# Attention and gated feed-forward on one core: one batch of attention, and chunk 0 alone, ahead of the fast chunks

## The chip, the cores and the metric

One core of one Trainium2 chip. The metric is the device time of one launch in microseconds (us), on the chip; several executions of each kernel were timed, and medians are quoted. The span of a profile is a little shorter than the timed run that it belongs to (1127.2 against 1129.3 us for the kernel before), so spans are compared with spans and timed runs with timed runs. The outputs of all kernels below were correct.

## The reference

```python
def _attn_ref(q, k, v, g_norm):                     # (8 batches, 8 heads, 576, 64), float32
    kv = np.einsum('bhsd,bhse->bhde', k, v)
    out = np.einsum('bhsd,bhde->bhse', q, kv)
    rms = np.sqrt(np.mean(out * out, axis=-1, keepdims=True) + 1e-06)
    return (out / rms * g_norm).astype(np.float32)

def _moe_ref(x, w_gate, w_val, w_out):              # 4608 tokens, d_model 512, d_ff 1536
    gate = 1.0 / (1.0 + np.exp(-(x @ w_gate)))
    val = x @ w_val
    return (gate * val @ w_out).astype(np.float32)

# x of the second is the first's result, heads side by side; the three weights are float64
```

## The kernel before

Words used below:

- A **pair** is two heads of attention. A batch has four pairs. A pair's steps on TensorE are kv (k times v), q (transposes of q), u (q times kv) and x (transposes of the normed u); each is followed by a step of ScalarE or VectorE. The last one, `x_out`, writes the pair's part of `xT`, the input of the feed-forward.
- A **chunk** is 512 tokens, nine in all. Chunk 0 needs batch 0 alone, chunk 1 batches 0 and 1.
- A **unit** is 1024 float64 weights in each of 128 partitions, which VectorE (DVE) and ScalarE (ACT) turn into float32 in five **conversion steps**: 12 units of gate and value weights (one for each f of 128 columns of d_ff), then 6 of w_out.
- A **block** (c, f) is the first layer of chunk c for one f: eight 512-column matmuls, then a sigmoid of the gate half on ACT and the product of both halves on DVE.
- "**Seven products**" is a Strassen-like scheme of the later chunks: seven quarter-size products in place of eight, for some added and subtracted quarters (of x on DVE, of the gate and value weights on GpSimd (POOL), of w_out once).
- A **slot** is a place between two matmuls at which one waiting step of the next batch's attention, or one sum, is emitted. Every engine takes its instructions in the order in which they are emitted.
- **Half clock**, or a **cold** array: stretches in which PE takes twice as long for like work. The same ten u records took 2.48 us early in the kernel after and 1.26 later (10.57 and 28.71 us); at full clock the array is called **warm**. The **granted clock** of a view is 1.00 at full and 0.50 at half clock.

The order in which the conversion steps are queued, each turn of a block, and the old plan: eight pairs, then chunks 0 and 1 block by block.

```python
    halves_of = [convert(u) for u in range(len(units))]   # per unit: ([s0, s1], [s2, s3, s4])
    converts, last = deque(), {}
    converts.extend(halves_of[0][0] + halves_of[0][1] + halves_of[1][0])
    last[0] = 5
    for u in range(1, len(units)):
        if u + 1 < len(units):
            converts.extend(halves_of[u + 1][0])
        converts.extend(halves_of[u][1])
        last[u] = len(converts)
    # ... (convert_some(n) emits the next n steps; s0, s1: a DVE step and an ACT step each;
    #      s2, s3, s4: DVE alone; s4 also starts the load of a later unit)

    def plain(c, f, n_convert, ps):
        converted(f)
        blk = Plain(c, f, ps)
        for at in range(2 * NMT):                         # eight matmuls
            i, m = divmod(at, NMT)
            blk.mm(i, m)
            slot()
            if late:
                late.popleft()()                          # gate and product of the block before
            convert_some(n_convert * (at + 1) // 8 - n_convert * at // 8)
        late.extend([blk.gate, blk.end])

    def stage(i, n_convert):                              # four pairs under way at a time
        do(i, KV, Q, KV_OUT, Q_OUT)
        do(i - 2, U_SUM, U_ROOT, U_NORM)
        do(i - 1, U, U_SQUARE)
        do(i - 3, X, X_OUT)
        convert_some(n_convert)

    for i in range(NE + 1):                               # NE = 8 pairs
        stage(i, 2 if i < 2 else 1 if i == 2 else 0)
    # ... block (0, 0), the last pair's last steps
    blocks = [(1, 0)] + [(c, f) for f in range(1, NFT - 3) for c in range(2)] + [(0, f) for f in range(NFT - 3, NFT)]
    for n, (c, f) in enumerate(blocks):
        plain(c, f, 5, halves(two(n % 4)))
    finish()
    convert_some(len(converts))
    # ...
    tt(out=t2w[3], in0=b22, in1=b12, op=ALU.subtract)     # a sum of w_out's quarters
    feed(2, at_ps)                                        # queue batch 2's steps for the slots
    second_layer(0)                                       # t outermost, f innermost
    # ...
    for f in range(NFT - 3, NFT):
        plain(1, f, 0, (mm_ps(), mm_ps()))
        # ... the other three sums of w_out's quarters, the sums of the hidden layer
    flush()
    sums_of(2)
    second_layer_fast(1)                                  # seven products
    flush()
    for c in range(2, NG):
        if c + 1 < B:
            feed(c + 1, at_ps)
        first_layer_fast(c)                               # seven products
        sums_of(c + 1)
        second_layer_fast(c)
        flush()
```

## Time and profile before

| | kernel before |
|---|---|
| timed runs | 1130.72 us median of 3 (1128.84 to 1131.5) |
| span of the profile | 1127.2 us |
| eight pairs and blocks (0,0), (1,0) end, block (0,1) starts | 59.55 us |
| second layer of chunk 0 starts | 190.25 us |
| chunk 2 starts (from here on both kernels are the same) | 301.72 us |

The milestones are read from the chain of work that ended last: the first matmul of each part. The third stretch, from chunk 0's second layer to chunk 2, in columns: stretch, length, then busy time of TensorE (PE), its weight loads (PEld), DVE, ACT and POOL, granted clock, share of the DMA engines, GB/s:

```profile
190.25:301.72 111.47, 110.26 (x494) 70.09 (x493) 33.55 (x65) 24.50 (x42) 0.00 (x0) 1.00 0.19 49
```

PE loses 1.2 us of 111 here. So outside of the first 59.55 us the old kernel has nearly nothing left to win by better overlap; only work can be taken away.

### The profile page before, as it was taken

To read this page: it belongs to the slowest core of one execution; us is meant where nothing else is said; L and a number is where in the kernel's file an instruction comes from. 1 tells how busy PE (TensorE), PEld (TensorE's weight loads), DVE (VectorE), ACT (ScalarE), POOL (GpSimd) and SP (SyncE) were. 2 spreads that over 40 slices of the span, in tenths; PEclk is the share of its full clock that TensorE was granted. 3 is DMA by queue.
4 is the path that set the end of the run, shared out by engine and by line. 5 is a ranking of instruction groups with operands and counts; after the bars stand their busy time and mean duration, and the time that the engine had idled before them with its cause. 6 is when DMAs were issued, how large, how long until landed. Compare 5 with 4: busy or idle time off the path is not lost.

```text
span 1127.2 us, 14586 instructions
## 1 busy us (share of the span) xinstructions
PE 1106.3 (98%) x5616; PEld 884.9 (79%) x5616; DVE 536.6 (48%) x1087; ACT 310.5 (28%) x589; POOL 239.5 (21%) x342
## 2 busy tenths in 40 slices
PE   5999999999999999999999999999999999999998
PEld 5644444547888888888888888888888888888887
DVE  4577664054155524563355425551655246615641
ACT  3733330223033303331243113340334021101110
POOL 0000001000033303430133104420333034404420
PEclk9999999999999999999999999999999999999999
DMA  9944431220212012110202030201200000010001
GB/s 239 216 133 131 147 112 28 55 71 12 75 26 54 11 29 63 42 34 19 72 12 54 24 78 12 53 12 40 56 12 7 19 19 1 1 26 13 1 1 38
DMA packets 71588, 57.56 MB, mean 51 GB/s; under 512 B 40800, under 2 KB 65376, under 8 KB 71520
## 3 DMA queue, kind: packets, MB, share of 16 engines
q1 hardware_dynamic: 71360, 56.64, 19.1%
q8 instruction: 45, 0.74, 0.3%
q14 instruction: 23, 0.19, 0.1%
q10 hardware_dynamic: 160, 0.00, 0.0%
HBM read 47.19 MB, written 9.44 MB: 50 GB/s over the span
## 4 chain that ended last, share of the span: by engine, by line
PE 94%; DMA 2%; DVE 2%; ACT 1%; SPq 0%; issue 0%; DVEq 0%
PE mm L526 45%; PE mm L606 26%; PE two L400 9%; PE mm L385 4%; PE at L400 3%; PE at L256 2%; PE at L227 2%; DMA q<-in_q_dram 1%; PE at L241 1%; PE at L282 1%; PE mm L400 1%; DMA v<-in_v_dram 1%; PE two L256 0%; DVE sq L273 0%; DVE ms L264 0%; ACT gv L141 0%
## 5 line engine op out<-in xcount | busy, mean ns | idle before, releaser
L512 POOL TENSOR_TENSOR tw<-gv 128x256 f32<-128x256 f32 x168 | 120.7, 730 | 836.8 <-PE mm L526 655.6
L526 PE MATMUL mm<-sx,tw 128*128 128x256 f32 x672 | 159.7, 380 | 0.0
L526 PE MATMUL mm<-xT,tw 128*128 128x256 f32 x672 | 159.5, 380 | 0.0
L526 PE MATMUL mm<-xT,gv 128*128 128x256 f32 x672 | 158.7, 379 | 0.0
L526 PEld LDWEIGHTS mm<-xT,gv 128*128 128x128 f32 x672 | 127.7, 190 | 17.4
L526 PEld LDWEIGHTS mm<-sx,tw 128*128 128x128 f32 x672 | 126.1, 190 | 16.7
L526 PEld LDWEIGHTS mm<-xT,tw 128*128 128x128 f32 x672 | 125.3, 190 | 16.1
L512 POOL TENSOR_TENSOR tw<-gv,tw 128x256 f32<-128x256 f32 x168 | 123.8, 760 | 0.0
L400 PE MATMUL two<-xT,gv 128*128 128x512 f32 x256 | 111.3, 593 | 2.1 <-DVE gv L163 1.6
L400 PEld LDWEIGHTS two<-xT,gv 128*128 128x128 f32 x256 | 48.3, 190 | 62.4 <-issue 62.1
L606 PE MATMUL mm<-t2w,gv 128*128 128x256 f32 x384 | 89.0, 379 | 0.0
L606 PE MATMUL mm<-w,gv 128*128 128x256 f32 x384 | 88.1, 379 | 0.0
L606 PE MATMUL mm<-w,s 128*128 128x256 f32 x384 | 88.1, 379 | 0.0
L555 ACT ACTIVATE sg<-sg 128x256 f32<-128x256 f32 x84 | 35.0, 416 | 191.7 <-DVE sg L554 191.7
L606 PEld LDWEIGHTS mm<-w,s 128*128 128x128 f32 x384 | 73.0, 190 | 9.9
L606 PEld LDWEIGHTS mm<-t2w,gv 128*128 128x128 f32 x384 | 72.6, 190 | 9.7
L606 PEld LDWEIGHTS mm<-w,gv 128*128 128x128 f32 x384 | 72.5, 190 | 9.6
L526 PE MATMUL mm<-sx,gv 128*128 128x256 f32 x336 | 79.4, 379 | 0.0
L546 DVE TENSOR_TENSOR gv<-mm,sg 128x256 f32<-128x256 f32 x84 | 35.7, 425 | 88.9 <-PE mm L526 88.9
L533 ACT COPY sg<-mm 128x256 f32<-128x256 f32 x84 | 31.3, 372 | 141.0 <-PE mm L526 141.0
L526 PEld LDWEIGHTS mm<-sx,gv 128*128 128x128 f32 x336 | 63.1, 190 | 8.2
L562 DVE TENSOR_TENSOR gv<-gv,sg 128x512 f32<-128x512 f32 x84 | 67.2, 840 | 0.2
(93 smaller groups left out, 1151.0 us busy)
## 6 DMA issues: line engine op xcount, KB each, us to landing
k<-in_k_dram SPq DMA_DIRECT2D x32, 288.0 KB, 4.4
v<-in_v_dram SPq DMA_DIRECT2D x32, 288.0 KB, 5.1
q<-in_q_dram SPq DMA_DIRECT2D x64, 144.0 KB, 3.1
st<-in_moe_w_gate_dram SPq DMA_DIRECT2D x12, 512.0 KB, 3.9
st<-in_moe_w_val_dram SPq DMA_DIRECT2D x12, 512.0 KB, 5.3
st<-in_moe_w_out_dram SPq DMA_DIRECT2D x12, 512.0 KB, 4.0
out_dram<-sg SPq DMA_DIRECT2D x24, 192.0 KB, 2.3
out_dram<-sg SPq DMA_DIRECT2D x24, 128.0 KB, 2.3
```

The source lines that it names most:

```text
L227: nc.tensor.matmul(ps[HD * e:HD * e + HD, 0, 0:HD], pairs[n]["k"][:, e, js], pairs[n]["v"][:, e, js], start=(j == 0), stop=(j == NJ - 1))
L241: nc.tensor.transpose(ps[:, j // JH, c0:c0 + NP], pairs[n]["q"][:, j].rearrange("p e d -> p (e d)"), ident[0:NP, 0:NP])
L256: nc.tensor.matmul(d["u"][:, i], qT[:, M * i:M * i + MU], kvs[n % 2], start=True, stop=True)
L385: nc.tensor.matmul(ps, gv[c, f][:, P * t:P * t + P], w["wo", f], start=(f == 0), stop=(f == NFT - 1))
L400: nc.tensor.matmul(self.ps[i], w[("wg", "wv")[i], self.f][:, m, :], xT[self.c][:, m, :], start=(m == 0), stop=(m == NMT - 1), skip_group_c ...
L512: nc.gpsimd.tensor_tensor(out=tw[f, i], in0=b[in0], in1=b[in1] if isinstance(in1, tuple) else tw[f, in1], op=ALU.subtract)
L526: nc.tensor.matmul(ps, wt[:, m, :], xs[:, m, :], start=(new and m == 0), stop=(m == NK - 1), skip_group_check=True)
L533: nc.scalar.copy(out=d["sg"][:, h2], in_=pa)
L546: tt(out=d["h"][:, h2], in0=pb, in1=d["sg"][:, h2], op=ALU.add)
L555: nc.scalar.activation(out=d["sg"][:, h2], in_=d["sg"][:, h2], func=AF.Sigmoid)
L562: tt(out=d["h"], in0=d["h"], in1=d["sg"], op=ALU.mult)
L606: nc.tensor.matmul(ps, hs(f), ws[:, f, :], start=(new and f == 0), stop=(f == NF2 - 1), skip_group_check=True)
```

## The change

The intent is to take work from PE. Chunk 1's first layer was plain, because its blocks lay between chunk 0's as company for the conversion. Now chunk 0 alone goes with the conversion, and chunk 1 is the first of the fast chunks. So only batch 0 is needed before block (0,0), and batch 1 goes into the slots of chunk 0. The second layer of chunk 0 gets f outermost, since w_out is still being converted. The core of the diff:

```diff
-    NE = 2 * NHP
+    NE = NHP
...
-    converts.extend(halves_of[0][0] + halves_of[0][1] + halves_of[1][0])
-    last[0] = 5
-    for u in range(1, len(units)):
-        if u + 1 < len(units):
+    for u in range(len(units)):
+        if u <= 4:
+            converts.extend(halves_of[u][0])
+        if 4 <= u < len(units) - 1:
             converts.extend(halves_of[u + 1][0])
         converts.extend(halves_of[u][1])
...
-            slot()
+            if at % 2:
+                slot()
             if late:
                 late.popleft()()
-            convert_some(n_convert * (at + 1) // 8 - n_convert * at // 8)
+            if 0 < at < 7:
+                convert_some(1)
...
-    for i in range(NE + 1):
-        stage(i, 2 if i < 2 else 1 if i == 2 else 0)
... (the start, now pair by pair:)
+    do(0, KV, Q, KV_OUT, Q_OUT, U, U_SQUARE, U_SUM, U_ROOT)
+    convert_some(2)
+    do(0, U_NORM, X, X_OUT)
+    convert_some(1)
+    do(1, KV, Q, KV_OUT, Q_OUT, U, U_SQUARE)
+    convert_some(2)
+    do(1, U_SUM, U_ROOT)
+    do(2, KV, Q, KV_OUT, Q_OUT)
+    do(1, U_NORM)
+    blk.mm(0, 0)
...
-    blocks = [(1, 0)] + [(c, f) for f in range(1, NFT - 3) for c in range(2)] + [(0, f) for f in range(NFT - 3, NFT)]
-    for n, (c, f) in enumerate(blocks):
-        plain(c, f, 5, halves(two(n % 4)))
+    plain(0, 1)
+    feed(1, at_ps)
+    for f in range(2, NFT):
+        plain(0, f)
+    ps = [mm_ps() for _ in range(G // P)]
+    for f in range(NFT - 2):
+        if f % 2 == 0:
+            converted(NFT + f // 2)
+        for t in range(G // P):
+            second(t, f)
+            if t % 2:
+                slot()
+            ...
+            if t < 3:
+                convert_some(1)
+    flush()
+    convert_some(len(converts))
...
+    fill.extend(x_sums(1))
... (second(t, f) for the last two f, copies and stores)
+    def t2w_sum(i, in0, in1):
+        for fs in (slice(0, NF2 // 2), slice(NF2 // 2, NF2)):
+            fill.append(lambda fs=fs: tt(out=t2w[i][:, fs], in0=in0[:, fs], in1=in1[:, fs], op=ALU.subtract))
+    t2w_sum(3, b22, b12)
+    t2w_sum(1, b12, b11)
+    t2w_sum(2, b22, t2w[1])
+    t2w_sum(4, b21, t2w[2])
-    for c in range(2, NG):
+    for c in range(1, NG):
```

More of the change, by code (lines that the diff above doesn't have):

```diff
@@ L64 @@
     first = first_ctx.__enter__()
-    NE = 2 * NHP
+    NE = NHP
     pairs = {n: {} for n in range(B * NHP)}
-    def ahead(n, late):
-        return (n + 4,) if n + 4 < NE else (n + late,) if n + late >= NE else ()
     def load_kv(n):
@@ L163, in s4 @@
             vec.tensor_tensor(out=m, in0=m, in1=d["p"].bitcast(FP32), op=ALU.mult)
-            if u:
-                load_next_unit()
+            load_next_unit()
         return [s0, s1], [s2, s3, s4]
@@ L187, in converted @@
         convert_some(last[u] - made[0])
-    for n in range(4):
+    for n in range(NE):
         load_kv(n)
@@ L193 @@
             load_next_unit()
+    load_next_unit()
+    load_next_unit()
     w2 = const.tile([P, NFT, DM], FP32, name="w2")
@@ L233, in kv_out @@
                 nc.vector.tensor_copy(out=kvs[n % 2][es, es], in_=d["kv"][es, 0, 0:HD])
-            for i in ahead(n, 2):
-                load_kv(i)
+            if n + 2 >= NE:
+                load_kv(n + 2)
         def q_mm():
@@ L246, in q_out @@
             nc.scalar.copy(out=d["qT"], in_=d["q"][:, :, 0:JH * NP])
-            for i in ahead(n, 1):
-                load_q(i)
+            if n + 1 >= NE:
+                load_q(n + 1)
         def u_mm():
@@ L358, in at_ps, with early, ps @@
         return psum_at.tile([P, 2, 512], FP32, tag="at", name="at")
-    def two(i):
-        return at_ps(None) if i == 3 else psum0.tile([P, 2, 512], FP32, tag=f"two{i}", name="two")
-    shared = [None]
-    turns = {"u": 1, "qx": 0}
-    def early(kind):
-        if kind == "q":
-            return shared[0]
-        tag = "u" if kind == "u" else "qx"
-        t = two(turns[tag] if tag == "u" else 2 + turns[tag])
-        turns[tag] = 1 - turns[tag]
-        if kind == "kv":
-            shared[0] = t
-            return t[:, :, JH * P:]
-        return t
+    def early(n):
+        shared = []
+        def ps(kind):
+            if kind == "q":
+                return shared[0]
+            t = psum0.tile([P, 2, 512], FP32, tag="kq" if kind == "kv" else f"ux{n % 2}", name="two")
+            if kind == "kv":
+                shared.append(t)
+                return t[:, :, JH * P:]
+            return t
+        return ps
     def mm_ps():
         return psum.tile([P, 512], FP32, tag="mm", name="mm", bufs=6)
-    def second_layer(c):
-        for t in range(G // P):
-            ps = mm_ps()
-            for f in range(NFT):
-                nc.tensor.matmul(ps, gv[c, f][:, P * t:P * t + P], w["wo", f], start=(f == 0), stop=(f == NFT - 1))
-                if f % 2:
-                    slot()
-            ot = sg_tile()
-            nc.scalar.copy(out=ot, in_=ps)
-            store(c, t, ot)
     class Plain:
@@ L410, with plain @@
     late = deque()
-    def finish():
-        while late:
-            late.popleft()()
-    def halves(t):
-        return t[:, 0], t[:, 1]
-    def plain(c, f, n_convert, ps):
+    def plain(c, f):
         converted(f)
-        blk = Plain(c, f, ps)
+        blk = Plain(c, f, (mm_ps(), mm_ps()))
         for at in range(2 * NMT):
@@ L425, in plain @@
             blk.mm(i, m)
-            slot()
+            if at % 2:
+                slot()
             if late:
                 late.popleft()()
-            convert_some(n_convert * (at + 1) // 8 - n_convert * at // 8)
+            if 0 < at < 7:
+                convert_some(1)
         late.extend([blk.gate, blk.end])
     KV, KV_OUT, Q, Q_OUT, U, U_SQUARE, U_SUM, U_ROOT, U_NORM, X, X_OUT = range(11)
-    a = [attention(n, early) for n in range(NE)]
+    a = [attention(n, early(n)) for n in range(NE)]
@@ L436, in do @@
     def do(n, *steps):
-        if 0 <= n < NE:
-            for step in steps:
-                a[n][step]()
-    def stage(i, n_convert):
-        do(i, KV, Q, KV_OUT, Q_OUT)
-        do(i - 2, U_SUM, U_ROOT, U_NORM)
-        do(i - 1, U, U_SQUARE)
-        do(i - 3, X, X_OUT)
-        convert_some(n_convert)
-    for i in range(NE + 1):
-        stage(i, 2 if i < 2 else 1 if i == 2 else 0)
-        if i + 5 == NE:
-            load_next_unit()
-            load_next_unit()
-    blk = Plain(0, 0, halves(early("u")))
@@ L454 @@
-    for m in range(NMT):
-        blk.mm(0, m)
-    do(NE - 1, U_SUM, U_ROOT)
-    do(NE - 2, X, X_OUT)
-    do(NE - 1, U_NORM)
-    convert_some(2)
-    for m in range(2):
-        blk.mm(1, m)
-    do(NE - 1, X, X_OUT)
-    for m in range(2, NMT):
-        blk.mm(1, m)
-    convert_some(2)
-    blk.gate()
+        for step in steps:
+            a[n][step]()
+    at0 = at_ps(None)
+    blk = Plain(0, 0, [at0[:, i] for i in range(2)])
+    do(0, KV, Q, KV_OUT, Q_OUT, U, U_SQUARE, U_SUM, U_ROOT)
@@ new lines @@
+    convert_some(2)
+    do(0, U_NORM, X, X_OUT)
+    convert_some(1)
+    do(1, KV, Q, KV_OUT, Q_OUT, U, U_SQUARE)
+    convert_some(2)
+    do(1, U_SUM, U_ROOT)
+    do(2, KV, Q, KV_OUT, Q_OUT)
+    do(1, U_NORM)
+    blk.mm(0, 0)
+    do(2, U, U_SQUARE, U_SUM, U_ROOT)
+    do(1, X, X_OUT)
+    blk.mm(1, 0)
+    do(3, KV, Q, KV_OUT, Q_OUT)
+    do(2, U_NORM)
+    blk.mm(0, 1)
+    do(3, U, U_SQUARE, U_SUM, U_ROOT)
+    do(2, X, X_OUT)
+    blk.mm(1, 1)
+    convert_some(1)
+    do(3, U_NORM)
@@ L467 @@
+    blk.mm(0, 2)
+    blk.mm(1, 2)
+    do(3, X, X_OUT)
+    convert_some(4)
+    blk.mm(0, 3)
+    blk.mm(1, 3)
+    late.extend([blk.gate, blk.end])
     first_ctx.__exit__(None, None, None)
     hp = ctx.enter_context(tc.tile_pool(name="hp", bufs=21))
-    blk.end()
-    blocks = [(1, 0)] + [(c, f) for f in range(1, NFT - 3) for c in range(2)] + [(0, f) for f in range(NFT - 3, NFT)]
-    for n, (c, f) in enumerate(blocks):
-        plain(c, f, 5, halves(two(n % 4)))
-    assert n % 4 == 3
-    finish()
@@ L475, with second @@
-    convert_some(len(converts))
     psum_ctx.__exit__(None, None, None)
     psum = ctx.enter_context(tc.tile_pool(name="psum", bufs=1, space=bass.MemoryType.PSUM))
+    plain(0, 1)
[3 more added lines that the diff above has]
+    ps = [mm_ps() for _ in range(G // P)]
+    def second(t, f):
+        nc.tensor.matmul(ps[t], gv[0, f][:, P * t:P * t + P], w["wo", f], start=(f == 0), stop=(f == NFT - 1),
+                         skip_group_check=True)
+    for f in range(NFT - 2):
[5 more added lines that the diff above has]
+                slot()
+            if late:
+                late.popleft()()
+            if t < 3:
+                convert_some(1)
@@ L635 @@
     sums = ctx.enter_context(tc.tile_pool(name="sums", bufs=2, side="right"))
+    for n in (1, 2, 3, 4):
+        for f in (0, NF2):
+            w_sum(f, n)
+    fill.extend(x_sums(1))
+    for t in range(G // P):
+        for f in range(NFT - 2, NFT):
+            second(t, f)
+            slot()
+        ot = sg_tile()
+        nc.scalar.copy(out=ot, in_=ps[t])
+        store(0, t, ot)
     b12, b11, b21, b22 = (w2[:, NF2 * (j - 1):NF2 * j, DH * (n - 1):DH * n] for j, n in ((1, 2), (1, 1), (2, 1), (2, 2)))
@@ L638 @@
     t2w[1] = b12
-    tt(out=t2w[3], in0=b22, in1=b12, op=ALU.subtract)
-    feed(2, at_ps)
-    second_layer(0)
-    for n in (1, 2, 3, 4):
-        for f in (0, NF2):
-            w_sum(f, n)
-    for f in range(NFT - 3, NFT):
-        plain(1, f, 0, (mm_ps(), mm_ps()))
-        if f == NFT - 3:
-            tt(out=t2w[1], in0=b12, in1=b11, op=ALU.subtract)
-            tt(out=t2w[2], in0=b22, in1=t2w[1], op=ALU.subtract)
-            tt(out=t2w[4], in0=b21, in1=t2w[2], op=ALU.subtract)
-            for i in range(NF2 - 3):
-                h_sums(1, i)
-    finish()
-    for i in range(NF2 - 3, NF2):
-        h_sums(1, i)
-    flush()
-    sums_of(2)
-    second_layer_fast(1)
-    flush()
-    for c in range(2, NG):
+    def t2w_sum(i, in0, in1):
[6 more added lines that the diff above has]
+    for c in range(1, NG):
         if c + 1 < B:
```

## The prediction

> **What bounds the kernel now.** I read the page first (busy shares, slices), then the chain of waits, then the stretches between its milestones, then the timeline of the first 75 us.
>
> ```profile
> PE 1106.3 (98%) x5616; PEld 884.9 (79%) x5616; DVE 536.6 (48%) x1087; ACT 310.5 (28%) x589; POOL 239.5 (21%) x342
> PE   5999999999999999999999999999999999999998
> DVE  4577664054155524563355425551655246615641
> ```
>
> TensorE (PE) is busy in 98% of 1127.2 us, and only its first slice is thin. So time is won by less PE work, or by less PE idling at the start. The chain gives the milestones: block (0,1), the first that needs weight unit 1, starts at 59.55; chunk 0's second layer at 190.25; chunk 2 at 301.72. From there on the two kernels have the same program, 825.5 us long.
>
> ```profile
> 0.00:59.55 59.55, 43.74 (x393) 32.89 (x393) 30.21 (x59) 31.28 (x58) 0.70 (x6) 1.00 0.93 216
> 59.55:190.25 130.70, 130.70 (x305) 57.99 (x306) 86.59 (x97) 42.32 (x49) 5.52 (x8) 1.00 0.34 112
> 301.72:422.53 120.81, 120.81 (x685) 106.56 (x685) 56.87 (x130) 34.98 (x71) 33.43 (x48) 1.00 0.16 39
> ```
>
> The columns are the stretch, its length, busy time of PE, PEld, DVE, ACT, POOL, clock, DMA share, GB/s. The first 59.55 us lose 15.8 us of PE; the 19 blocks after them lose none. A chunk by seven products with one batch of attention takes 120.81 us.
>
> The conversion stretch holds the warning for this change:
>
> ```profile
> 59.32 0.69 DVE L139 TENSOR_SCALAR gv<-st 128x1024 uint32<-128x1024 uint32 x1
> 60.04 1.15 ACT L141 ACTIVATE gv<-gv,one 128x1024 f32<-128x1024 uint32 x1 [4.89 <-DVE gv L139]
> 61.09 1.13 ACT L149 ACTIVATE cz<-cz,exp_off 128x1024 int32<-128x1024 uint32 x1
> 62.13 0.58 ACT L405 ACTIVATE sg<-two 128x512 f32<-128x512 f32 x1
> 62.74 0.69 DVE L408 TENSOR_TENSOR gv<-two,sg 128x512 f32<-128x512 f32 x1 [2.13 <-ACT sg L405]
> 63.35 1.22 DVE L154 SCALAR_TENSOR_TENSOR gv<-st,gv 128x1024 f32<-128x1024 uint32 x1
> 66.88 0.69 DVE L139 TENSOR_SCALAR gv<-st 128x1024 uint32<-128x1024 uint32 x1
> ```
>
> One unit's turn through VectorE (DVE) and ScalarE (ACT) takes 66.88 - 59.32 = 7.56 us, of which DVE works about 5.4 and waits 2.13: the gate's activation stands behind two conversion activations in ACT's order, and the block's product on DVE behind the gate. A block of eight 512-column matmuls takes PE 6.87. Before, this turn being longer than a block costs nothing: each unit serves two blocks, and four two-bank PSUM tiles let PE run ahead.
>
> **What the Trainium skill says.** (1) "TensorE: Matmul & The Clock Gate", Part 1: the array starts at half clock and is released after a busy window of about 3.4 us. The trace agrees: 24 key-value matmul records took 1.55 us at 17.27 and 0.92 at 20.50, after unbroken work from 12.44. (The page's PEclk row reads 9 throughout and doesn't show it.)
>
> ```profile
> 17.27 1.55 PE L227 MATMUL two<-v,k 96*64 96x64 f32 x24
> 20.50 0.92 PE L227 MATMUL at<-v,k 96*64 96x64 f32 x24
> ```
>
> (2) The same page, "Architectural detail": ACT and DVE are strict FIFOs. The waits above are that; nothing overtakes. (3) "ScalarE: Activation LUTs", "What ACT_TABLE_LOAD costs": 1283 ns and a drain of 1380 at each switch of set. The trace has the 1283 but no such drain: at 53.26 a load starts 0.01 after the activation before it, and the gate starts 0.01 after the load.
>
> **The change part by part.** A 512-column fp32 matmul is two records and costs PE 0.859 us (6.87/8); a 256-column one 0.432 (72.52 us for 168 in chunk 7's first layer, the chain's 905.77 to 978.29).
>
> *Chunk 1 by seven products.* Plain: 12 x 8 x 0.859 = 82.4 us. Seven products: 72.5. **PE loses 9.9 us of work.** Everything else of PE is kept: chunk 0's second layer is 48 x 0.859 = 41.2 in either order of its loops. The four sums of w_out's quarters (1.76 us each on DVE, three of them beside the last plain blocks) become eight halves in chunk 1's slots; DVE is busy 56.9 of 120.8 us there, so I give them nothing. Chunk 1 should take 120.8.
>
> *The start.* Before, it was transfers: eight head pairs and units 0 to 2, with the eighth pair's q landing at 36.9. Now four pairs and unit 0 precede (3.5 + 1.05 MB). At the 3.6 us per pair and 3.3 per unit at which the first ones landed, pair 3 is in at 21.5, unit 1 at 25, unit 2 at 28. Transfers therefore no longer set the start. But the new instruction order is nearly serial: PE's queue is kv0 q0 u0 x0 kv1 q1 u1 kv2 q2 m u2 x1 m kv3 q3 m u3 x2 m m m x3 m m, where before a pair's five steps were spread over four stages. I followed the queues with the durations of before (kv 0.92, q 0.71, u 1.27, x 0.66 warm and 1.55, 1.15, 2.1, 1.1 cold; square 0.70, sum 0.82, root 0.30, reciprocal 0.22, norm 0.82, qT 0.64, kv copy 0.46, three xT pieces 1.04; 0.03 for a semaphore, 0.14 to PE):
> - u0 11.0 to 13.2, norm0 ends 17.1 behind a table load and unit 0's first two steps, x0 17.3 to 18.3, kv1 and q1 to 21.0, u1 22.3 to 24.4 (all cold, PE idles too much);
> - from about 25.5 warm: u2 to 29.3, q3 to 32.5, u3 33.9 to 35.1, sum3 to 36.7, root3 to 37.05;
> - ACT's queue has xT of pair 2 only after root3, 37.05 to 38.1, then unit 1's first activation to 39.2, then xT of pair 3, 40.4 to 41.4, then unit 1's second to 42.5; so DVE's steps 3 and 4 of unit 1 end at 43.75 and 44.9.
>
> **Block (0,1) starts at about 45**, 14.5 us before its old time. By then one block is done, where before there were two and four more pairs.
>
> *Chunk 0 alone.* PE alone would need 11 x 6.87 = 75.6, about 10.5 for the part of batch 1 that lies in these slots, so 131 for the second layer's start. But each block now carries six conversion steps (1.2 units, 5.8 us of DVE), its own product (0.61) and a third of a pair (2.3/3 = 0.77): 7.2 of DVE against 7.9 of PE. With the waits of DVE for a gate that stands behind conversion activations and table loads, DVE takes more than PE. Following the queues block by block, its idle ahead of the products or sums is 1.7, 2.1, 1.0, 3.4, 1.7, 0.8, 0, 1.3, 2.3, 1.3, about 15.6 us in all. PE may run ahead only as far as batch 1's steps allow, since they share one PSUM tile: I find it waiting 0.35 and 0.65 for units 5 and 6, 1.8 for qT of pair 5, and 4.3 for xT of pair 6, whose activations are queued behind those of unit 15. The second layer then starts at 139.5 instead of 131. It carries three steps per f (2.9 us of DVE in 3.44 of PE) and should not wait: 41.2 and 1.9 of attention end it at 182.6.
>
> *Sum.* Chunk 2 starts at 182.6 + 120.8 = 303.4, against 301.72: **1.7 us later**, so a span of about 1129. The timed run was 3.5 us over the profile's span, which gives 1132. My chain in the start assumed every step serial, so I take 1131. In one line: -9.9 of PE work, about +12 of PE waiting, namely the start's remaining idle and 7 us in chunk 0's blocks.
>
> **The rivals.**
> - *PE stays the bound in chunk 0* (conversions keep up). For it: DVE was 66% busy in the old stretch and sums to less than PE's time. Then the second layer starts at 131 and the span is about 1120, 1124 timed. Against it: the 7.56 turn above.
> - *DVE's turn is a full 7.56 per unit, plus attention, everywhere.* With 1.2 units and 0.8 of attention a block would take 8.9 to 9.2 instead of 8.6, the second layer would start 4 to 6 us later still: 1137. For it: each turn of before shows the wait; against: six steps per block shift the gate to another place in the turn each time.
> - *Transfers bind in the stretch.* A unit's buffer is free at the end of step 3, its load lands some 6.2 us later (0.9 issue, 5.3 landing), and batch 1's loads queue with it on SP. Between the freeing and the need lies a turn plus 1.2 us, about 8; I find each landed 1 to 6 us ahead. If attention's loads hold one up, 2 to 5 us more: 1135.
> - *Clock.* If PE is warm from 20 us, the start is 2 us shorter; if cold to 30, 2 longer.
>
> **Range and chances.** These alternatives go from 1122 to 1138 and are nearly independent; 8 in 10 for 1120 to 1141. Over 2% faster means below 1108, which needs no waits at all in the blocks and also a start 12 us shorter than I find: 0.04. Over 2% slower means above 1153, twice the waits found: 0.03. Within 2%: 0.93.
>
> **What would show it.** Right: first-layer busy time of PE less by some 10; block (0,1) at 43 to 47; blocks of 8 to 9 us in which PE waits for ACT's qT or xT steps or for DVE's step 4, and DVE's product waits for its gate; second layer from 136 to 143; chunk 1 in 121 us; chunk 2 from 298 to 308. Wrong: block (0,1) well before 42 (the start isn't serial), PE without waits from there to the second layer (the rival), DVE's first steps ended by the landing of a unit (transfers), or chunk 1 well over 121 (the quarter sums are not free).

## The result, and the profile after

| | before | after |
|---|---|---|
| timed runs | 1130.22 us median of 4 (1128.84 to 1131.5) | 1135.82 us median of 4 (1134.27 to 1135.99) |
| span of the profile | 1127.2 | 1134.2 |
| block (0,1) starts | 59.55 | 45.50 |
| second layer of chunk 0 starts | 190.25 | 139.80 |
| chunk 1's fast first layer starts | none | 185.04 |
| chunk 2 starts | 301.72 | 308.75 |
| from there to the end of the span | 825.48 | 825.45 |

The ratio after/before is 1.0047, with a 95% interval of 1.0029 to 1.0064. A ratio here is the mean time of one kernel's fast runs over that of the other's of the same rounds, so it is not quite the ratio of the medians quoted. The time is the same within 2%, as predicted, and in fact longer by half a per cent.

The whole page after shows little, and that is worth seeing:

```profile
PE 1104.0 (97%) x5760; PEld 914.0 (81%) x5760; DVE 569.0 (50%) x1155; ACT 328.3 (29%) x621; POOL 279.2 (25%) x390
```

PE's busy time fell by 2.3 us only (1106.3 to 1104.0), where the change removes 9.9. Busy time counts a matmul at half clock at twice its length, so lost clock hides in this sum. The stretches tell more (columns as above):

```profile
0.00:45.50 45.50, 27.91 (x196) 20.00 (x197) 19.26 (x36) 19.11 (x32) 0.70 (x6) 1.00 0.81 203
45.50:139.80 94.30, 87.42 (x342) 42.92 (x342) 76.53 (x96) 51.50 (x63) 0.00 (x0) 0.99 0.59 180
139.80:150.00 10.20, 10.20 (x28) 5.06 (x27) 7.51 (x10) 4.38 (x5) 0.00 (x0) 0.76 0.39 126
139.80:185.04 45.24, 45.24 (x113) 20.72 (x112) 20.82 (x22) 10.11 (x14) 8.02 (x8) 0.95 0.14 41
185.04:308.75 123.71, 121.86 (x686) 106.36 (x685) 66.52 (x136) 33.97 (x71) 37.54 (x48) 1.00 0.15 40
```

PE idles 17.6 us of the first 45.5 (45.50 less 27.91), 6.9 of the eleven blocks, and 1.85 of chunk 1, where PE was never idle in a fast chunk of the kernel before (120.81 of 120.81 us, in the prediction's lines). In the second layer it idles nowhere, but the granted clock is 0.76 in its first 10 us.

**Where PE waits in the blocks.** The timeline of PE alone, in columns start, length, engine, line, operation, output and inputs, and in brackets the idle time before it and what ended it:

```profile
85.52 1.98 PE L383 MATMUL mm<-xT,gv 128*128 128x512 f32 x4 [0.82 <-DVE gv L160]
88.87 1.35 PE L254 MATMUL at<-kv,qT 128*116 128x128 f32 x10 [1.36 <-ACT qT L244]
138.78 1.22 PE L239 MATMUL at<-ident,q 96*128 96x96 f32 x6 [4.70 <-ACT xT L289]
139.80 6.04 PE L461 MATMUL mm<-w,gv 128*128 128x512 f32 x8
```

The longest wait is that of pair 7's q, 4.70 us. Its cause is in the order of ACT and DVE in the time before it (timeline of all engines, some lines left out):

```profile
131.89 0.69 DVE L391 TENSOR_TENSOR gv<-mm,sg 128x512 f32<-128x512 f32 x1 [1.99 <-ACT sg L388]
...
135.62 1.15 ACT L138 ACTIVATE w<-w,one 128x1024 f32<-128x1024 uint32 x1 [3.76 <-DVE w L136]
136.67 1.13 ACT L146 ACTIVATE cz<-cz,exp_off 128x1024 int32<-128x1024 uint32 x1
...
137.71 1.02 ACT L289 ACTIVATE xT<-at,g_col 128x345 f32<-128x345 f32 x3
...
138.62 0.60 ACT L388 ACTIVATE sg<-mm 128x512 f32<-128x512 f32 x1
...
139.63 0.68 DVE L391 TENSOR_TENSOR gv<-mm,sg 128x512 f32<-128x512 f32 x1
```

PE had given `xT` of pair 6 its input by 130.6 (the transposes, 0.66 us from 129.98), and ACT was idle from 131.86. But `xT` and the last block's gate (L388) stand in ACT's queue behind two activations of a w_out unit, and the first of these waits 3.76 us for DVE. DVE, in turn, had itself waited 1.99 us for the gate before, and had two longer steps of the unit before to do first. Pair 7's q needs the PSUM tile `at` that `xT` empties. When PE goes on, it does so at half clock: the first eight records of the second layer take 6.04 us in this view (5.83 in the chain, which leaves out the overlap with the step before), where eight at full clock take 3.6 (as in run x6_five below). The trace's clock record has half clock from 137.8 to 144.6 us.

**Chunk 1.** The halves of w_out's quarter sums (L653) on DVE beside the weight differences (L511) on POOL, timeline of all engines:

```profile
189.97 0.95 DVE L653 TENSOR_TENSOR w<-w 128x768 f32<-128x768 f32 x1
...
196.11 1.50 DVE L653 TENSOR_TENSOR t2w<-w 128x768 f32<-128x768 f32 x1
196.76 2.13 POOL L511 TENSOR_TENSOR tw<-gv 128x256 f32<-128x256 f32 x2
...
198.20 1.50 DVE L653 TENSOR_TENSOR t2w<-w,t2w 128x768 f32<-128x768 f32 x1
...
204.92 1.97 PE L525 MATMUL mm<-xT,tw 128*128 128x256 f32 x8 [0.70 <-DVE gv L537]
```

A half sum takes 0.95 us with POOL idle (189.97; POOL's first difference comes at 193.06) and 1.31 to 1.50 while POOL works. PE waits in this stretch twice for DVE's L537 (1.0 us in all), an addition that frees a PSUM tile, and once for a copy of kv (0.8).

**The balance up to chunk 2**, worked out with a 512-column matmul at 0.859 us, a 256-column one at 0.432, and 3.0 us of PE for a pair, all at full clock. What is left of a stretch after this work is its loss, idle or half clock:

| | before | after |
|---|---|---|
| start, to block (0,1) | 59.55 - 8 pairs (24.0) - 2 blocks (13.75) = 21.8 | 45.50 - 4 pairs (12.0) - 1 block (6.87) = 26.6 |
| blocks to the second layer | 0 | 94.30 - 11 blocks (75.6) - attention (10.4) = 8.3 |
| second layer of chunk 0 | (in the next line) | 45.24 - 41.2 - attention (1.6) = 2.4 |
| the rest, to chunk 2 | 1.3 | 123.71 - 120.81 = 2.9 |
| **loss in all** | **23.1** | **40.2** |

So 10 us of work went, 17 us of loss came, and chunk 2 starts 7.0 us later. The whole difference of the spans is 7.0.

### The profile page after: what moved, and what is told of

Its sections match the earlier page's. It is cut to its first block, busy times and chain, and to the rows that moved or that the text cites. A ratio compares the mean times of both kernels' runs of the same rounds, so it can differ in the third digit from the quotient of the medians.

```text
span 1134.2 us, 15099 instructions
## 1 busy us (share of the span) xinstructions
PE 1104.0 (97%) x5760; PEld 914.0 (81%) x5760; DVE 569.0 (50%) x1155; ACT 328.3 (29%) x621; POOL 279.2 (25%) x390
## 4 chain that ended last, share of the span: by engine, by line
PE 89%; DVE 6%; ACT 3%; issue 2%; DMA 0%; SPq 0%; DVEq 0%; ACTq 0%
PE mm L525 50%; PE mm L605 26%; PE mm L461 4%; PE at L254 3%; PE at L225 2%; PE at L239 1%; DVE cz L155 1%; PE at L280 1%; DVE gv L151 1%; PE mm L383 1%; PE two L254 1%; DVE gv L136 1%; ACT cz L146 1%; DVE gv L391 0%; PE two L225 0%
## 5 line engine op out<-in xcount | busy, mean ns | idle before, releaser
L511 POOL TENSOR_TENSOR tw<-gv 128x256 f32<-128x256 f32 x192 | 139.4, 737 | 804.1 <-PE mm L525 640.0
L525 PE MATMUL mm<-xT,tw 128*128 128x256 f32 x768 | 182.4, 380 | 1.0 <-DVE gv L537 1.0
L525 PE MATMUL mm<-sx,tw 128*128 128x256 f32 x768 | 182.4, 380 | 0.0
L525 PE MATMUL mm<-xT,gv 128*128 128x256 f32 x768 | 181.6, 379 | 0.0
L525 PEld LDWEIGHTS mm<-xT,gv 128*128 128x128 f32 x768 | 145.5, 190 | 20.1 <-issue 0.5
L525 PEld LDWEIGHTS mm<-xT,tw 128*128 128x128 f32 x768 | 143.3, 190 | 20.2 <-issue 1.8
L525 PEld LDWEIGHTS mm<-sx,tw 128*128 128x128 f32 x768 | 144.1, 190 | 19.0
L511 POOL TENSOR_TENSOR tw<-gv,tw 128x256 f32<-128x256 f32 x192 | 145.2, 778 | 0.0
L383 PE MATMUL mm<-xT,gv 128*128 128x512 f32 x176 | 78.4, 596 | 2.7 <-DVE gv L160 2.7
L541 ACT ACTIVATE sg<-mm 128x256 f32<-128x256 f32 x96 | 36.3, 383 | 99.6 <-PE mm L525 99.6
```

The lines of the kernel that those rows point to most:

```text
L383: nc.tensor.matmul(self.ps[i], w[("wg", "wv")[i], self.f][:, m, :], xT[self.c][:, m, :], start=(m == 0), stop=(m == NMT - 1), skip_group_c ...
L511: nc.gpsimd.tensor_tensor(out=tw[f, i], in0=b[in0], in1=b[in1] if isinstance(in1, tuple) else tw[f, in1], op=ALU.subtract)
L525: nc.tensor.matmul(ps, wt[:, m, :], xs[:, m, :], start=(new and m == 0), stop=(m == NK - 1), skip_group_check=True)
L541: nc.scalar.activation(out=d["sg"][:, h1], in_=pa, func=AF.Sigmoid)
```

## The experiments

The theory after the result: the work is gone as meant, and three things take the gain: the serial start, ACT's order in the blocks (with the cold clock that the longest wait leaves), and the quarter sums in chunk 1. The main rivals: that the waits move on when one is removed, that DVE's load as such is the bound in the blocks, and that a cold clock, not the order, costs the time. All ratios are to the kernel before in the same rounds. All outputs are right. Spans are compared with 1134.2 (after), one profiled execution each. Other executions of one kernel differ by up to 3.4 us, and the ratios give somewhat smaller gains over after than the spans: 0.41% or 4.6 us for x1_gap (6.1 by span), 5.2 for x3_start (6.1), 7.8 for x6_five (9.9), 12.8 for x4_all (14.0). The intervals of x2_t2w and x8_warm overlap with that of after, so these two are read from stretches inside the profile, not from the whole time.

### x1_gap: move pair 7's q (and pair 5's) three slots back

```diff
+                if steps is two_:
+                    fill.extend([lambda: None] * gap)
...
-    feed(1, at_ps)
+    feed(1, at_ps, 3)
```

> Edit: in batch 1 of the attention, three empty slots (about 5.2 us of PE) stand ahead of the second pair's q step, twice; nothing else. Theory (PE is held in chunk 0 by the one PSUM tile that batch 1's steps share, whose release waits in ACT's queue behind conversion activations): the waits of 1.36 us for pair 5's qT and of 4.70 us for pair 6's xT go, and with the latter the half-clock start of the second layer (2.3 us); the second layer starts at 132 to 135 instead of 139.8, the span is 1126 to 1129 instead of 1134.2. Rival (DVE's total work in chunk 0 is the bound, the shared tile only shows where it becomes visible): PE waits as long at other places, for the last step of a unit, and the span stays within 2 us of 1134.

Measured: span 1128.1 (6.1 less), 1130.16 us median, ratio 1.0006 (0.9987 to 1.0025). The second layer starts at 135.08 and runs warm:

```profile
135.08:178.92 43.84, 43.84 (x123) 20.73 (x122) 23.22 (x27) 14.99 (x21) 5.50 (x8) 1.00 0.19 59
```

The 4.70 wait is gone and the clock is 1.00. Of the 6.1, 4.7 is the earlier start of this stretch, and 1.4 its shorter length (45.24 in after), though more of the attention falls into it. DVE still waits 15.2 us for gates in the blocks (13.1 in after), and two smaller PE waits grew (0.82 to 1.43 for a unit's step 4, 1.36 to 2.04 for qT of pair 5). So one wait on ACT, with the cold clock after it, cost some 6 us; the rival's "waits move on" is true of 1.3 us.

### x2_t2w: the quarter sums in the second layer of chunk 0 instead of chunk 1

```diff
-    for f in range(NFT - 2):
+    def second_f(f):
...
+    for f in range(NFT // 2):
+        second_f(f)
 ... (t2w_sum(3 ...), t2w_sum(1 ...), t2w_sum(2 ...), t2w_sum(4 ...) queued here)
+    for f in range(NFT // 2, NFT - 2):
+        second_f(f)
+    flush()
```

> Edit: the eight half sums of w_out's quarters are put into chunk 0's second layer after its sixth f, where DVE is idle for 22 us, instead of chunk 1's first eight slots. Theory (these eight sums are what made chunk 1 2.9 us longer than the 120.8 us of the other chunks): chunk 1 takes 120.8 to 121.3 us and the span is 1131 to 1132, 2.5 to 3 less. Rival (chunk 1 is longer because of POOL's first weight differences or anything else of a first chunk): chunk 1 stays at 123 to 124 and the span within 1 us of 1134.

Measured: span 1131.8 (2.4 less), 1132.33 us, ratio 1.0023 (1.0008 to 1.0038). Chunk 1:

```profile
185.34:306.30 120.96, 120.96 (x686) 106.71 (x685) 56.41 (x129) 36.82 (x73) 33.38 (x48) 1.00 0.16 41
```

PE is busy the whole stretch, and its waits for L537 and for kv are gone; DVE has 10.1 us less to do than in after (66.52) and POOL 4.2 less. So the sums did cost chunk 1 its 2.8 us, and no other cause is needed there. They are not faster in the second layer (0.96 to 1.47 us each; there too POOL works beside them), but PE waits for nothing there: the second layer takes 45.22, as in after (45.24).

### x3_start: the start of before, with four pairs

```diff
-    do(0, KV, Q, KV_OUT, Q_OUT, U, U_SQUARE, U_SUM, U_ROOT)
-    convert_some(2)
-    do(0, U_NORM, X, X_OUT)
 ... (the serial order goes, and the pairs share PSUM tiles as in the kernel before)
+    for i in range(NE + 1):
+        do(i, KV, Q, KV_OUT, Q_OUT)
+        do(i - 2, U_SUM, U_ROOT, U_NORM)
+        do(i - 1, U, U_SQUARE)
+        do(i - 3, X, X_OUT)
+        convert_some(2 if i < 2 else 1 if i == 2 else 0)
```

> Edit: only the order of the start: the first batch's four pairs run in the stages of the kernel before (a pair's steps spread over four stages, key-value and q of the next pair ahead of u of this one, four PSUM tiles), then block 0 with unit 1's conversion beside it. Loads unchanged. Theory (the start is long because a pair's steps follow one another in PE's, DVE's and ACT's queues, with PE at half clock in the gaps): block (0,1) starts at 31 to 35 us instead of 45.5, and the span falls by 9 to 13 us, to 1121 to 1125, if the later stretch keeps its length. Rival (the start is set by the landing of the weight units): block (0,1) is not earlier than 42 and the span within 3 us of 1134.

Measured: span 1128.1 (6.1 less), 1130.27 us, ratio 1.0001 (0.9986 to 1.0016). The timeline of PE:

```profile
27.60 1.32 PE L254 MATMUL two<-kv,qT 128*116 128x128 f32 x10 [1.98 <-DVE sq L271]
...
39.65 8.85 PE L387 MATMUL mm<-xT,gv 128*128 128x512 f32 x20 [1.41 <-DVE gv L395]
```

Block (0,1) starts at 39.65, 5.85 us earlier, and everything later keeps its waits to the hundredth (0.82, 1.36, 4.70). So the start of before, with its order and its PSUM tiles, is worth 6 us. That it is the order is shown by x7_five below, which keeps the tiles of after and starts block (0,1) at 38.82. My expectation of 9 to 13 was too high: in the staged order u of pair 2 waits 1.53 and u of pair 3 waits 1.98 for norms on DVE (there are only two u tiles, and a norm frees one), and block (0,1) waits 1.41 for block (0,0)'s product.

### x4_all: x1_gap, x2_t2w and x3_start together

Its diff is the three above.

> The three edits that each gave something together: empty slots ahead of the second pairs' q in batch 1 (-6.1 us alone), quarter sums in the second layer (-2.4), staged start (-6.1). Theory (they act at separate places of one path, so they add): span 1134.2 - 14.6 = 1119.6, 1118 to 1122, thus 0.993 of the kernel before. Rival (a quicker start only brings transfers and DVE forward against each other in chunk 0): span 1123 or more.

Measured: span 1120.2, 1121.87 us, ratio 0.9934 (0.9917 to 0.995). The three gains are 6.1 + 2.4 + 6.1 = 14.6, and the three together gave 14.0. They add up: three separate causes, one after the other in time, on the one engine that sets the end.

### x5_inner: f innermost in the second layer

```diff
-    for f in range(NFT - 2):
-        if f % 2 == 0:
-            converted(NFT + f // 2)
-        for t in range(G // P):
+    for t in range(G // P):
+        for f in range(NFT if t < 3 else NFT - 2):
+            if t == 0 and f % 2 == 0:
+                converted(NFT + f // 2)
```

> Edit: chunk 0's second layer with f innermost (one 128-row tile after the other), which undoes that part of the change; conversions are drawn forward with it as far as the first tile needs them. Theory (f outermost lets the second layer begin while w_out is still being converted): the first tile gets to its last f some 10 us after 139.8 while the last unit's conversion takes until 153 to 158, so PE waits 4 to 9 us there, span 1138 to 1143. Rival (the conversions run far enough ahead, the order is worth nothing): span within 1 us of 1134.

Measured: span 1139.3 (5.1 more), 1141.08 us in its one execution. PE:

```profile
151.12 2.62 PE L461 MATMUL mm<-w,gv 128*128 128x512 f32 x4 [2.35 <-DVE w L160]
154.65 9.36 PE L461 MATMUL mm<-w,gv 128*128 128x512 f32 x16 [0.91 <-DVE w L160]
```

PE waits for w_out's units, 3.3 us in all, and both waits are followed by half clock: four records take 2.62 us where four at full clock took 1.98 (85.52 in after), and sixteen take 9.36, where sixteen at full clock take 6.9 (16 x 0.43, an estimate). Chunk 1 starts at 190.10 instead of 185.04. So f outermost is worth about 5 us here, waits and lost clock together: this part of the change does what it is for. The difference is larger than the spread of any kernel's runs here (up to 3.4 us), but the run stands alone.

### x6_five: five conversion steps per block, each unit's five in order

```diff
-        if u <= 4:
-            converts.extend(halves_of[u][0])
-        if 4 <= u < len(units) - 1:
-            converts.extend(halves_of[u + 1][0])
-        converts.extend(halves_of[u][1])
+        converts.extend(halves_of[u][0] + halves_of[u][1])
...
-            if 0 < at < 7:
+            if 0 < at < 6:
```

> Edit: five conversion steps per block instead of six, and each unit's five steps in order, so that two units are never interleaved; a block then carries just one unit. Theory (DVE falls behind PE because, six steps a block and the next unit's two activations ahead of the gate, each turn through DVE and ACT is longer than a block of PE): ACT has a unit's activations done in mid block, DVE's waits for a gate shrink from up to 3.6 us to about 1, the 4.70 us wait for pair 6's xT and the half-clock start of the second layer go; PE waits 1 to 3 us in all between block (0,1) and the second layer, which starts at 132 to 135 instead of 139.8; span 1126 to 1129 instead of 1134.2. Rival (a unit's own two latencies through ACT, now bare on DVE, make the turn as long as before; or the second layer runs into w_out's conversion, which has lost its lead): PE waits for a unit's last step at every block or in the second layer, span 1132 or more.

Measured: span 1124.3 (9.9 less), 1127.04 us, ratio 0.9978 (0.9963 to 0.9993). The waits of the blocks (who waited for whom: us in total, times, longest), first in after, then in x6_five:

```profile
DVE gv L391 <- ACT sg L388: 13.1, 7, 3.6
```

```profile
DVE gv L387 <- PE mm L379: 9.8, 10, 1.8
```

and PE's timeline in x6_five:

```profile
124.28 3.70 PE L379 MATMUL mm<-xT,gv 128*128 128x512 f32 x8 [0.67 <-DVE gv L160]
...
132.25 3.63 PE L457 MATMUL mm<-w,gv 128*128 128x512 f32 x8
```

In after, DVE's product waits 13.1 us for the gate, which has stood behind conversion activations. In x6_five the product waits for PE instead: DVE is ahead, and PE, the engine that sets the end, is the one waited for. PE's own waits behind DVE and ACT between block (0,2) and the second layer shrink to 0.67. The second layer starts at 132.25 (7.55 earlier), the 4.70 wait never comes, and its first eight records take 3.63. What is not told apart: the edit changes both the number of steps in a block and their order, and eleven steps fewer are in the blocks (DVE 67.6 us busy in 86.9, instead of 76.5 in 94.3). A rival in which DVE's load per block alone is the cause is not excluded; the waits by themselves show that the gate's wait went.

### x8_warm: extra identity matmuls in the gaps of the start

```diff
+    def warm(n):
+        for _ in range(n):
+            nc.tensor.matmul(at0[:, 0, 0:P], ident, ident, start=True, stop=True, skip_group_check=True)
+    warm(14)
+    do(0, KV, Q)
+    warm(16)
+    do(0, KV_OUT, Q_OUT, U)
+    warm(24)
...
+    do(1, KV, Q)
+    warm(8)
```

> Edit: 62 matmuls of 128 columns on the identity, whose results nobody reads, in the gaps of PE's queue in the start (before the first key-value product, after q and u of pair 0, after q of pair 1); nothing else. Theory (in the start of the changed kernel PE works at half clock until about 27 us because of its gaps, and in a serial chain each slow step counts): u of pairs 0 and 1 take 1.3 us instead of 2.5, the key-value products 0.9 instead of 1.55; block (0,1) starts 3 to 5 us earlier, at 41 to 43, span 1129 to 1131. Rival (the start hangs on DVE, ACT and transfers, PE's clock lies beside them): block (0,1) within 1 us of 45.5 or later by the extra matmuls.

Measured: span 1131.3 (2.9 less), 1133.47 us, ratio 1.0032 (1.0017 to 1.0047). u of pair 0 in after, then in x8_warm:

```profile
10.57 2.48 PE L254 MATMUL two<-kv,qT 128*116 128x128 f32 x10 [2.56 <-ACT qT L244]
```

```profile
12.50 1.25 PE L254 MATMUL two<-kv,qT 128*116 128x128 f32 x10
...
138.10 4.79 PE L472 MATMUL mm<-w,gv 128*128 128x512 f32 x8
```

The same work at half its length: with enough matmuls ahead, u runs at full clock. But the extra matmuls hold up kv of pair 0 (7.50 instead of 5.30), so block (0,1) comes only 1.7 us earlier. The other 1.2 us have another cause, which I had not foreseen: after the very same 4.70 wait, the first eight records of the second layer took 4.79 instead of 6.04 (both in the timeline). The clock records of the two traces show the difference: half clock lasts 3.41 us here, from 137.0 to 140.4, and 6.83 us in after, exactly twice as long. The other three executions of x8_warm have a mean clock of 0.997, as the profiled one of after has, against 0.998 here; so the 1.2 us look like chance of this execution and not like a gain of the edit. The ratios fit that, though their intervals overlap: x8_warm's is 0.15% below after's, 1.7 us, no more than the start's gain. As tried here, then, warming gained 1.7 us, net of the 2.2 by which the extra matmuls hold up pair 0; the other order gained 5.85 (x3_start).

### x9_plain1: chunk 1's first layer plain again

```diff
-    fill.extend(x_sums(1))
...
-        first_layer_fast(c)
+        if c == 1:
+            for f in range(NFT):
+                plain(1, f)
+                if f > NF2:
+                    h_sums(1, f - NF2 - 1)
+            ...
+        else:
+            first_layer_fast(c)
```

> Edit: chunk 1's first layer by plain blocks of eight 512-column matmuls, as in the kernel before, which undoes that part of the change and leaves the rest. Theory (PE work of 12 x 8 x 0.859 = 82.4 us against 168 x 0.432 = 72.5, and PE is the bound in chunk 1): chunk 1 takes 9 to 10 us longer than without the quarter sums' waits, 130 to 133 us, span 1141 to 1144. Rival (in chunk 1 the seven products' extra DVE and POOL work eats most of what PE saves): span 1135 to 1138.

Measured: span 1141.2 (7.0 more), 1142.5 us, ratio 1.0112 (1.0095 to 1.0129). Chunk 1:

```profile
184.86:315.53 130.67, 130.67 (x542) 79.28 (x541) 35.19 (x72) 29.82 (x49) 0.00 (x0) 1.00 0.14 37
```

Plain, chunk 1 takes 130.67 without any wait. By seven products it takes 120.96 where the quarter sums lie elsewhere (x2_t2w), 9.7 less, against the 9.9 predicted; with them in it (after) 123.71. So the part of the change that saves work saves what it should, and gives 2.8 of it back at once.

### x7_five and x7_warm: the parts that helped, put together

x7_five is x6_five and x2_t2w with a tighter start: the steps of two pairs interleave, and a pair's sum comes right after the next pair's q.

```diff
 ... (x6_five's and x2_t2w's edits)
-    do(0, KV, Q, KV_OUT, Q_OUT, U, U_SQUARE, U_SUM, U_ROOT)
-    convert_some(2)
-    do(0, U_NORM, X, X_OUT)
+    do(0, KV, Q)
+    do(0, KV_OUT, Q_OUT, U, U_SQUARE, U_SUM, U_ROOT)
+    do(1, KV, Q)
     convert_some(1)
-    do(1, KV, Q, KV_OUT, Q_OUT, U, U_SQUARE)
+    do(0, U_NORM)
+    do(1, KV_OUT, Q_OUT)
+    do(0, X, X_OUT)
+    do(1, U, U_SQUARE)
...
```

> Three edits to beat both kernels: five conversion steps a block in strict order (-9.9 alone), quarter sums in the second layer (-2.4), and a tighter order of the start (pair n+1's key-value and q products ahead of pair n's transposes, sums as soon as their squares are there, unit 1's first two steps in the wait for the last root). Theory: block (0,1) at 36 to 38 us, PE without waits over 1 us from there to the end; span 1134.2 - 9.9 - 2.4 - 8.5 = 1113.4, 1111 to 1117, 0.988 of the kernel before. Rival (unit loads then bind in the blocks, since each unit's five steps wait for its own landing): DVE's first steps wait for transfers, span 1118 or more.

Measured: span 1115.2, 1116.73 us median (1116.32 to 1119.68), ratio 0.9891 (0.9874 to 0.9908). PE:

```profile
34.00 0.69 PE L276 MATMUL two<-ident,sq 115*128 115x115 f32 x5 [0.98 <-DVE sq L267]
...
38.82 1.45 PE L379 MATMUL mm<-xT,gv 128*128 128x512 f32 x3
```

Block (0,1) starts at 38.82 (expected 36 to 38), so the start gave 6.7 of the 8.5 expected; and from 30 us to 300 PE waits for another engine only twice, this 0.98 and once 0.7. It beats both kernels: 1.1% below before, so still within 2% of it.

x7_warm adds ten identity matmuls between q and u of pair 0:

```diff
+    do(0, KV, Q)
+    warm(10)
+    do(0, KV_OUT, Q_OUT, U, U_SQUARE, U_SUM, U_ROOT)
```

> The same with ten matmuls on the identity between q and u of pair 0. Theory (PE's gap there, 2.5 us, delays the full clock; the rest of this start is dense): u of pair 0 at full clock or full clock by 15 us, block (0,1) 1 to 2 us earlier than without, span 1111 to 1113. Rival (the start hangs on ACT and DVE): no change beyond 0.5 us, or later by the time that the ten take.

Measured: span 1115.6, 1116.92 us, ratio 0.9887 (0.9873 to 0.9902): no change. u of pair 0 took 1.25 instead of 2.48, but PE fell back (u of later pairs at 2.23 and 2.38, half clock), and block (0,1) starts at 39.25.

## Why the prediction was right

The class (within 2%) and the range (1120 to 1141) hold; the time was 1135.8 instead of 1131. By its own steps:

- **Less work by seven products, 9.9 us:** right. 9.7 between x9_plain1 and x2_t2w.
- **The serial start, block (0,1) at about 45:** right, 45.50. Its loss is 26.6 us, more than that of the old start (21.8) although half the pairs are in it; x3_start and x7_five, with the same loads, reach 39.65 and 38.82, so the order and not the transfers costs these 6 us.
- **Waits in the blocks, second layer at 139.5:** right, 139.80. I gave PE waits of 0.35 and 0.65 for units 5 and 6, 1.8 for qT of pair 5 and 4.3 for xT of pair 6; measured were one of 0.82 for a unit's step 4, 1.36 and 4.70. Named waits of 7.1 don't make up the 8.5 by which I put the start later (131 to 139.5); the 1.4 left over had no term. Measured were 8.3 of loss with 6.9 of waits; of the rest, 0.56 is pair 7's q at half clock (1.22 for 0.66), and what the other 0.8 are stays open. The mechanism, a gate and an attention step behind conversion activations, is read from ACT's timeline; x1_gap shows what the longest wait is worth, and x6_five that the gate's wait on DVE goes with another order and number of steps.
- **Second layer 41.2 + 1.9, "should not wait":** it didn't wait, yet took 45.24 instead of 43.1. The term left out is the clock: it fell at 137.8, inside the very wait that I had predicted (4.3, measured 4.70). With the wait gone (x1_gap, x6_five) the clock is 1.00 there.
- **Chunk 1 in 120.8, "I give them nothing" for the quarter sums:** this term was wrong by 2.9 (2.75 by x2_t2w). I had added up DVE's busy time and found room; but the sums lengthen beside POOL's work (0.95 to 1.50) and stand in DVE's queue ahead of the sums that free PE's PSUM tiles.
- **The sum.** "-9.9 of PE work, about +12 of PE waiting": the work was 10 less, and the loss 17 more; 2.4 of the missing 5 are the second layer's clock, 2.9 the quarter sums. The last step, from 1132 to 1131 since "my chain in the start assumed every step serial", went the wrong way: the start was as serial as assumed. And the 3.5 us from span to timed run were the old kernel's median less the span of one execution, which was itself timed 2.1 over its span; for the kernel after, the same difference is 1.6. So 1.9 of the 5.3 us missed in the chain don't show in the time, by luck. And "within 2%", 23 us here, was easy to hit: the mechanism is tested by the milestones, not by it.
- **The rivals.** PE as the bound in chunk 0 (1124): false here; it comes true in x6_five. A full turn of 7.56 everywhere (1137): near in time, for another reason, since the second layer began when the theory said. (Its own sum doesn't come out either: 1.2 x 7.56 is 9.1 before any attention, where 8.9 to 9.2 was said to include 0.8 of it.) Transfers: none of PE's waits in the blocks ended by one. Clock, given 2 us either way in the start: it mattered in another place.

So the expected 10 us were lost again to a new wait on ACT with its cold clock (6.1 by x1_gap), to the serial order of a start that could have been 6.1 shorter (x3_start), and to sums laid into DVE's queue at the wrong place (2.4 by x2_t2w). Not settled: whether in x6_five it is the order or the number of steps that counts.

## What to carry to other kernels

When work is taken off an engine that was never idle, look first at what kept it busy: the company of chunk 1's blocks was what made the conversion's turns free, and without it, late activations became waits of PE (6.9 us in the eleven blocks, none in the nineteen before). In engines that take their instructions in order, emit a step that the bound engine needs ahead of a long step that itself still waits for its input; here the place of one attention step was worth some 6 us (x1_gap), and another order together with one step fewer in a block 9.9 (x6_five). Room in the sum of an engine's busy time isn't room at a given place: 10 us of DVE work cost 2.8 us of PE in a stretch in which DVE was half idle, and none in another.

## What the Trainium skill lacked or had wrong

- "TensorE: Matmul & The Clock Gate", Part 1 (the clock falls after an idle window of some 3.4 us, and the window runs freely): agrees with the 4.70 us wait and the half clock after it, which lasts 3.41 us in x8_warm and 6.83 in after, about one window and two. The page's 500 ns either way are for the transition in its own test; after the same wait here, the first eight records differ by 1.25 us (4.79 against 6.04). In x5_inner the clock fell at 152.3 us, although PE had waited for 2.35 us only (until 151.12), so a wait shorter than a window was enough.
- The same page warns, under "Seeing it yourself", that the clock events of a trace have been seen to be unreliable. It doesn't name the case found here: the clock record of a trace begins with the first change, in after at 28.6 us, and the view gives 1.00 for all that comes before, where u of pair 0 took 2.48 us instead of 1.25. Durations of like instructions are the safer sign.
- "SBUF — State Buffer", SBUF: two separate sides (a DVE instruction with two SBUF inputs and a GpSimd one that reads SBUF exclude each other on a shared port, and the later one is blocked for the whole of the other's instruction): in line with the runs, where a half sum took 0.95 us alone and up to 1.50 beside POOL's differences, but no run here removes POOL's work alone. The page's figures are for other pairs of instructions; here the cost was up to 0.55 us for each half sum.
- "ScalarE: Activation LUTs", What ACT_TABLE_LOAD costs: the prediction's finding stands, 1.28 us for a load and no drain of 1.38 beside it. In after the gate starts 0.02 us after a load ends (79.32 + 1.28, next at 80.62).
- No page has the cost of two coupled in-order queues, an ACT step that waits for DVE ahead of an ACT step that DVE waits for: 13.1 us of DVE's waiting in the eleven blocks here.
